# A DeltaNet and SwiGLU kernel: first diagonals with heads side by side, ScalarE's passes over the first weight piece ahead of its copies of N, and the last stores on two queues

## The chip, the cores and the metric

The kernel runs on one core of a Trainium2 chip. The metric is the device time of one execution in microseconds; lower is better. A core has five engines that run side by side and meet only through semaphores: TensorE (PE, with its weight loads PEld), VectorE (DVE), ScalarE (ACT), GpSimd (POOL) and SyncE (SP), which here only issues transfers. A transfer (DMA) is issued on the queue of SP, ACT or POOL and is carried by 16 shared DMA engines.

## The reference

A gated-delta-rule attention block feeds a SwiGLU feed-forward block. Only this matters here:

```python
k_n = k / (np.linalg.norm(k, axis=-1, keepdims=True) + 1e-06)     # q, k, v: (4, 8, 768, 48)
for t in range(S):
    y[:, :, t] = np.einsum('bhd,bhde->bhe', q[:, :, t], state)
    v_old = np.einsum('bhde,bhd->bhe', state, kt)
    state = state + bt[:, :, :, None] * np.einsum('bhd,bhe->bhde', kt, vt - v_old)
x = y.transpose(0, 2, 1, 3).reshape(3072, 384)
g = x @ w_gate                                                    # (384, 1536)
out = (g * (1.0 / (1.0 + np.exp(-g))) * (x @ w_val)) @ w_out      # (1536, 384)
```

Inputs q, k, v and beta are float32, the three weight matrices are float64, and the output is float32.

## The kernel before

The sequence is cut into 12 chunks of 64 tokens. Inside a chunk the recurrence is turned into matrix products: the Gram matrices of the k rows (and of q with k) on TensorE, a triangular inverse, and products with the state, which is carried from chunk to chunk. With a batch of 4 and 8 heads there are 32 matrices of 64 by 64 in a chunk, 16 in each half of the partitions. A matrix is cut into blocks of 32 rows, and the inverse is built from blocks: the diagonal blocks are inverted by a substitution on VectorE that steps through all heads together, and the blocks below the diagonal come in through matrix products with a matrix called N.

The start. The order of the instructions on each engine is the order of the program from line 1929 on; nothing is reordered by a scheduler. Chunks 0 and 1 are treated apart:

- `load_k(0)` and `load_k(1)` (line 190) put half of each transfer on SP's queue and half on ACT's. All other loads are on SP's queue, apart from beta's eight small ones on POOL's (`load_beta`, line 406).
- `norms` (line 381) squares and sums the k rows on VectorE and takes the root on POOL. Between the square and the sum of chunk 0 stands a memset of `qpad[0]`'s padding (line 388). `load_q(0)`, the first transfer of SP's queue behind the k rows of chunks 0 and 1, writes `qpad[0]` and so waits for that memset. Behind it on SP's queue stand k of chunks 2 and 3, q of 1, v of 0, q of 2, and then the weight pieces.
- `turned` (line 461) transposes a chunk's rows on TensorE into PSUM; ScalarE copies them to SBUF (line 488 or 490).
- `first_gram` (line 639) makes the Gram matrices of a chunk, 32 products of 64 columns, into two PSUM banks, one for each parity of the head. In a bank the 512 columns of a row are x (which 32 of the 64 columns), then the head, then i, so that the 32 columns of one head lie side by side. For chunk 1 the two banks are those that its transposes came out of.
- `first_diag` (line 650) picks the diagonal blocks: ScalarE multiplies the first half by a row mask (line 654), VectorE adds the second half with another (line 656). They go to `first_of["flat"]`, where the 32 columns of one i hold all heads of both chunks; an element of one head is thus written 32 elements (128 bytes) behind the last.
- VectorE transposes `flat` (line 1951), which is what `first_substitution` (line 691) works on, 30 instructions in a row. `first_z` (line 710) transposes the result back, `spread_z` (line 715) spreads it with one ScalarE instruction and three VectorE ones (lines 725 and 727), and `n_products` (line 729) makes N from it on TensorE (line 735).
- `low_copies` (line 665) copies the blocks below the diagonal from the same PSUM banks with 12 ScalarE instructions (line 669).
- `unread` (line 635) runs products that nobody reads, to keep TensorE busy while it would wait. Four of them (line 968 of the program) stand ahead of `n_products`.
- `first_advance` (line 942) is the recurrence's step for chunk 0: N's products, N's copies (`n_copies`, line 739, with lines 741 and 749), three chained products with N (line 954), the outputs of chunk 0, and at its end ScalarE's copy of the first state (line 1050). Chunk 1's step starts with a product on that state (line 1152).

The weights. They arrive as 64-bit numbers in pieces of 256 (later 512 or 384) columns, staged by `stage` (line 253) on SP's queue. Most of the first 18 pieces wait, by a copy of one column on POOL (line 261), for an earlier piece to have landed. `power_step` (line 266) makes two ScalarE passes over a piece (lines 274 and 280), and `convert` (line 284) three VectorE operations, which give the float32 values. `power_step(0)` stands behind the first step of `first_advance` (line 1993), so ScalarE makes its passes over piece 0 behind its copies of N and of the first products.

The rest. From chunk 2 on the feed-forward block of one chunk runs on TensorE while the next chunk's recurrence is fitted in between. `output_fast` (line 1667) makes the output of a chunk and stores the two halves of its tokens with `store` (line 1608), two transfers each on SP's queue. The last chunk's stores end the kernel.

Of the kernel before, what the change touches and what calls it, by code (L numbers as in the profile page):

```python
# [14 lines left out]
DP = 64  # L15
R = 32
# [4 lines left out]
def kernel(  # L21
# [25 lines left out]
    nc = tc.nc  # L47

    B, H, S, D = q.shape
    NCH = S // C  # L50
# [7 lines left out]
    HH = NB * H  # L58
# [38 lines left out]
    qpad = [const.tile([128, NB, H, DP], FP32, name=f"qpad{i}") for i in range(QB)]  # L97
# [283 lines left out]
    def norms(c):  # L381

        ksq = work.tile([128, NB, H, D], FP32, name="ksq", tag="r", bufs=2)
        x = knp[c][:, :, :, 0:D]
        nc.vector.tensor_tensor(out=ksq, in0=x, in1=x, op=ALU.mult)
        n = n_t[0][:, c].rearrange("p (par bp j) -> p par bp j", par=2, bp=NB)
        if c == 0:
            nc.vector.memset(qpad[0][:, :, :, D - 1 : DP], 0.0)
        ksq_v = ksq.rearrange("p bp (j par) d -> p par bp j d", par=2)
        for par in range(2):  # L390
            nc.vector.tensor_reduce(
                out=n[:, par], in_=ksq_v[:, par], axis=mybir.AxisListType.X, op=ALU.add
            )
        n = n_t[0][:, c]
        nc.gpsimd.tensor_tensor(out=n, in0=n, in1=half[:, 0:HH], op=ALU.pow)
# [58 lines left out]
    def banks(name, tag):  # L454

        if type(tag) is int:
            return [ps_ffn([128, 512], name, tag + i) for i in range(2)]
        p = ps_pair(name, tag)
        return [p[:, 0], p[:, 1]]

    def turned(c, of_q, tag=None):

        if tag is None:
            tag = "py" if of_q else "px"
        x = qpad[c % QB] if of_q else kn_of(c)
        if of_q:
            xt = work.tile([128, NB * NJ * 2 * C], FP32, name="qt", bufs=1)
        else:
            xt = kt_of(c)
        if c >= blocks_of[of_q][1]:  # L470
            xt_v = xt.rearrange("p (b bp j i) -> p bp j b i", bp=NB, b=2, j=NJ)
            (qt if of_q else kt)[c] = xt_v
            blocks = blocks_of[of_q][2]
            nc.vector.transpose(xt, blocks.rearrange("p bp h d -> p (bp h d)"))
            spent.append(1.8)
            if c + 1 < NCH:
                for par in range(2):
                    late_loads.append(lambda par=par: load_blocks(of_q, c + 1, (par,)))
            return
        xt = xt.rearrange("p (bp j b i) -> p bp j b i", bp=NB, j=NJ, b=2)  # L480
        (qt if of_q else kt)[c] = xt
        p_t = banks("p_t", tag)
        for bp in range(NB):
            for j in range(NJ):
                at = slice(128 * j, 128 * j + 128)
                nc.tensor.transpose(p_t[bp][:, at], x[:, bp, 2 * j : 2 * j + 2], ident)
            if type(tag) is int:
                nc.scalar.copy(xt[:, bp].rearrange("p j b i -> p (j b i)"), p_t[bp])
        for bp in range(NB if type(tag) is not int else 0):
            nc.scalar.copy(xt[:, bp].rearrange("p j b i -> p (j b i)"), p_t[bp])  # L490
        if of_q and c + QB < Q_BLOCKS:
            load_q(c + QB)
# [109 lines left out]
    first_of, l_sb, n_sb = {}, {}, {}  # L602
# [7 lines left out]
    def first_tiles():  # L610
        a = work.tile([128, C * 2 * HH], FP32, name="a_sb")
        for c in range(2):
            l_sb[c] = a[:, R * R * c : R * R * (c + 1)].rearrange(
                "p (h k) -> p h k", k=C
            )
        first_of["flat"] = new_mb().rearrange("p k i -> p (k i)")
        first_of["diag"] = first_of["flat"].rearrange("p (j h) -> p h j", j=R)
        first_of["zb"] = places["z1"].bitcast(FP32)[:, 4 * H_ - 1056 : 4 * H_]
        first_of["mb"] = places["wo"].bitcast(FP32)[:, 2 * H_ : 2 * H_ + 1056]
        nc.vector.memset(first_of["zb"], 0.0)  # L620
        for c in range(2):
            nc.vector.memset(l_sb[c][:, :, 48:C], 0.0)
        for x, rows in enumerate((slice(16, C), slice(R, C), slice(48, C), slice(0, R))):
            nc.vector.tensor_reduce(
                out=m_two[:, x],
                in_=ident.rearrange("p (b n) -> p b n", b=2)[:, :, rows],
                axis=mybir.AxisListType.X,
                op=ALU.add,
            )
        nc.vector.tensor_tensor(  # L630
            out=m_rows, in0=m_two[:, :, 0], in1=m_two[:, :, 1], op=ALU.add
        )
        nc.vector.tensor_scalar_mul(m_low, m_rows[:, 0:3], -1.0)
# [5 lines left out]

    def first_gram(c, tag):  # L640

        p_v = [p.rearrange("p (x h i) -> p x h i", x=2, i=R) for p in banks("p_g", tag)]
        for bp, j, par, b, _ in every():
            k_v = kt[c][half_of(par), bp, j, b].rearrange("p (x i) -> p x i", x=2)
            nc.tensor.matmul(
                p_v[par][half_of(b), :, NJ * bp + j], kt[c][half_of(par), bp, j, b], k_v
            )
        return p_v

    def first_diag(c, p):  # L650
        to = first_of["diag"][:, HH * c : HH * c + HH]
        to = to.rearrange("p (par h) j -> p par h j", par=2)
        for par in range(2):
            nc.scalar.mul(to[:, par], p[par][:, 0], m_rows[:, 3:4])
        for par in range(2):
            nc.vector.scalar_tensor_tensor(
                out=to[:, par],
                in0=p[par][:, 1],
                scalar=m_rows[:, 1:2],
                in1=to[:, par],  # L660
                op0=ALU.mult,
                op1=ALU.add,
            )
# [943 lines left out]

    def store(c, bp, o_sb):
        for b in range(2):
            nc.sync.dma_start(  # L1610
                out=out_v[NB * b + bp, c * C : (c + 1) * C],
                in_=o_sb[half_of(b)],
            )
# [172 lines left out]
    def step(kind, fn, *args):  # L1786
        key = (kind, args or (1,))
        if key not in gens:
            gens[key] = [fn(*args), 0]
        if next(gens[key][0], None) != MORE:  # L1790
            gens[key][1] += 1
# [128 lines left out]
    with tc.manual_schedule(  # L1920
# [8 lines left out]
        new_n(0)  # L1929
        load_beta()  # L1930
        first_tiles()
        norms(0)
        norms(1)
        load_q(0)
# [5 lines left out]
        unread(3, ps_pair("p_t", "px")[:, 0])  # L1940
        turned(0, False, 0)
        p_g = [first_gram(0, "px")]
        first_diag(0, p_g[0])
        turned(1, False, 2)
        p_g.append(first_gram(1, 2))
        first_diag(1, p_g[1])
        spread_beta(copy_a)
# [41 lines left out]
        new_nt(0, spare_of_q, state_flat[:, LEAD : LEAD + 512])  # L1989
        new_nt(1, zb_1.rearrange("p k i -> p (k i)"), spare_of_q[:, 0:512])  # L1990
        gens["advance", (0,)] = [first_advance(), 0]
        step("advance", advance, 0)
        power_step(0)
        step("advance", advance, 0)
        converts_first(0)
        power_step(2)
# [110 lines left out]
```

## Time and profile before

| what | value |
|---|---|
| median of 3 runs | 663.73 us (663.14 to 665.0) |
| the profiled execution, its own time | 662.01 us |
| its span (first to last instruction) | 660.3 us |
| TensorE busy | 647.3 us, 98% of the span |
| VectorE, ScalarE, GpSimd busy | 476.7, 281.5, 198.5 us |
| mean granted clock of TensorE | 0.997 |
| granted clock from 32.9 to 36.2 us | 0.50 |
| transfers | 68.57 MB, mean 104 GB/s |

The profiled execution is one run, and 1.72 us faster than the median of the three that were timed. Times in the views are microseconds from the start of its span. A line of the timeline has the start, the busy time, the engine, the source line, the operation, the tile written and the tile read, the shape and the number of instructions merged; in brackets stands how long the engine had been idle and what ended that. "issue" means that the profile shows nothing that was waited for. SPq and ACTq are the times in which an engine issues a transfer. TensorE's float32 products are made in two passes, so that the profile has two records of a product and two of its weight load.

### The profile page before, as it was taken

How to read it: one execution, taken by the hardware profiler on the slowest of the kernel's cores; microseconds unless marked ns; L12 is line 12 of the kernel's file. 1: busy time of each engine (PE TensorE's matmuls, PEld its weight loads, DVE VectorE, ACT ScalarE, POOL GpSimd, SP SyncE). 2: the span in 40 equal slices, each digit the busy share in tenths (PEclk: the TensorE clock that was granted, in tenths of full speed). 3: DMA queues.
4: the chain of work that ended last, by engine and by line, in shares of the span. 5: the costliest groups of instructions: out<-in, count | busy, mean ns of one | idle time of the engine just before them, and what ended most of it. 6: DMA issues, size and time to landing. Idle time of an engine off the chain costs nothing.

```text
span 660.3 us, 24914 instructions
## 1 busy us (share of the span) xinstructions
PE 647.3 (98%) x10856; PEld 595.8 (90%) x10856; DVE 476.7 (72%) x991; ACT 281.5 (43%) x626; POOL 198.5 (30%) x310
## 2 busy tenths in 40 slices
PE   8899999999999999999999999999999999999997
PEld 4568888767999999999999999999999999999997
DVE  6879799999688767758667758677758655655562
ACT  5788867124336433434433433532333433334230
POOL 7130041023894032880031881031881000000000
PEclk9999999999999999999999999999999999999999
DMA  9668762005742551373454274363363442222321
GB/s 135 142 173 272 205 164 101 1 14 99 195 81 69 103 117 51 93 140 84 104 127 88 61 164 92 85 135 98 72 136 85 100 105 66 62 94 66 87 66 25
DMA packets 147438, 68.57 MB, mean 104 GB/s; under 512 B 123456, under 2 KB 126560, under 8 KB 147328
## 3 DMA queue, kind: packets, MB, share of 16 engines
q1 hardware_dynamic: 144992, 66.48, 42.6%
q8 instruction: 85, 1.39, 0.8%
q10 hardware_dynamic: 2080, 0.39, 0.4%
q0 software_dynamic: 256, 0.10, 0.1%
q14 instruction: 25, 0.20, 0.1%
HBM read 59.08 MB, written 7.86 MB: 101 GB/s over the span
## 4 chain that ended last, share of the span: by engine, by line
PE 85%; DVE 6%; DMA 4%; SPq 2%; issue 1%; ACT 1%; POOL 0%; DVEq 0%; ACTq 0%; POOLq 0%
PE ffn L1407 40%; PE ffn L1683 21%; PE ffn L1564 8%; DMA h_f<-in_moe_w_val_dram 3%; PE ffn L1593 2%; PE p_px L1169 2%; SPq L139 2%; PE p_py L502 1%; DVE x_t L587 1%; DVE zb L593 1%; PE p_py L1071 1%; PE p_px L1152 1%; PE p_py L1088 1%; PE p_px L502 1%; PE p_px L923 1%
## 5 line engine op out<-in xcount | busy, mean ns | idle before, releaser
L1407 PE MATMUL ffn<-x_t,w_gv 128*128 128x128 f32 x800 | 108.7, 279 | 0.8 <-DVE p_sb L1633 0.7
L1407 PEld LDWEIGHTS ffn<-x_t,w_gv 128*128 128x128 f32 x800 | 97.4, 192 | 3.9 <-DVE p_sb L1633 1.8
L1441 ACT ACTIVATE sil<-ffn 128x256 f32<-128x256 f32 x100 | 36.4, 383 | 115.4 <-PE ffn L1407 109.3
L1407 PE MATMUL ffn<-x_ffn,w_gv 128*128 128x128 f32 x640 | 84.6, 275 | 0.0
L1683 PE MATMUL ffn<-wo_sb,h_f 128*128 128x192 f32 x480 | 83.9, 328 | 0.0
L1683 PEld LDWEIGHTS ffn<-wo_sb,h_f 128*128 128x128 f32 x480 | 77.9, 190 | 0.6
L1407 PEld LDWEIGHTS ffn<-x_ffn,w_gv 128*128 128x128 f32 x640 | 78.0, 192 | 0.3
L822 POOL TENSOR_TENSOR n_b<-mb,half 128x32 f32<-128x32 f32 x5 | 27.6, 5520 | 159.2 <-DVE mb L556 159.2
L587 POOL TENSOR_TENSOR h_f<-zb,mb 128x31 f32<-128x31 f32 (+15 forms) x124 | 69.3, 559 | 19.2 <-PE p_py L800 6.0
L593 POOL TENSOR_TENSOR zb<-zb,h_f 128x31 f32<-128x31 f32 (+15 forms) x124 | 70.6, 569 | 9.7
L1407 PE MATMUL ffn<-x_t,h_f 128*128 128x128 f32 x472 | 64.7, 280 | 0.0
L1407 PEld LDWEIGHTS ffn<-x_t,h_f 128*128 128x128 f32 x472 | 57.3, 192 | 1.6 <-DVE ffn L1633 0.5
L1442 DVE TENSOR_TENSOR h_f<-sil,ffn 128x256 f32<-128x256 f32 x100 | 39.3, 418 | 23.8 <-ACT sil L1441 23.8
L1103 ACT COPY x_ffn<-p_py 32x256 f32<-32x256 f32 (+3 forms) x108 | 39.3, 364 | 29.0 <-PE p_py L1088 27.3
L1633 DVE TENSOR_TENSOR ffn<-p_sb,ffn 128x512 f32<-128x512 f32 x40 | 27.8, 695 | 25.8 <-PE ffn L1407 25.1
L1636 DVE TENSOR_TENSOR ffn<-ffn,p_sb 128x512 f32<-128x512 f32 x40 | 27.5, 691 | 19.9 <-PE ffn L1407 19.1
L1683 PE MATMUL ffn<-last_k,h_f 128*128 128x192 f32 x200 | 36.0, 327 | 0.0
L1636 DVE TENSOR_TENSOR o_sb<-o_sb,ffn 128x192 f32<-128x192 f32 x50 | 17.5, 350 | 24.2 <-PE ffn L1683 23.7
L1564 PE MATMUL ffn<-x_t,w_gv 128*128 128x256 f32 x144 | 33.9, 385 | 0.2 <-DVE x_t L1045 0.2
L1683 PEld LDWEIGHTS ffn<-last_k,h_f 128*128 128x128 f32 x200 | 32.9, 190 | 0.1
L1564 PE MATMUL ffn<-x_ffn,w_gv 128*128 128x256 f32 x144 | 31.9, 380 | 0.0
L1407 PE MATMUL ffn<-x_ffn,h_f 128*128 128x128 f32 x232 | 30.9, 276 | 0.0
(330 smaller groups left out, 1172.7 us busy)
## 6 DMA issues: line engine op xcount, KB each, us to landing
h_f<-w_s SPq DMA_DIRECT2D x81, 256.0 KB, 2.8
more_w<-w_s SPq DMA_DIRECT2D x27, 256.0 KB, 2.8
vin<-in_v_dram SPq DMA_DIRECT2D x48, 96.0 KB, 3.5
out_dram<-o_sb SPq DMA_DIRECT2D x48, 96.0 KB, 2.2
kn<-in_k_dram SPq DMA_DIRECT2D x20, 192.0 KB, 4.7
zt<-in_moe_w_out_dram SPq DMA_DIRECT2D x10, 384.0 KB, 4.3
qpad<-in_q_dram SPq DMA_DIRECT2D x36, 64.0 KB, 3.0
w_s<-h_f SPq DMA_DIRECT2D x7, 256.0 KB, 2.8
```

What stands on the lines that cost most here:

```text
L139: dmas[b % len(dmas)].dma_start(out=t[64 * b : 64 * b + 64, :, :, 0:D].rearrange("p bp h d -> p (bp h) d"), in_=halves(x, c, b).rearrange( ...
L587: engine.tensor_tensor(out=t_v, in0=zb[:, 0 : j + 1, j : j + 1].to_broadcast([128, j + 1, m]), in1=mb[:, j : j + 1, j + 1 : R].to_broadcas ...
L593: engine.tensor_tensor(out=zb[:, 0 : j + 1, j + 1 : R], in0=zb[:, 0 : j + 1, j + 1 : R], in1=t_v, op=ALU.add,)
L822: nc.gpsimd.tensor_tensor(out=n, in0=mb.rearrange("p j i -> p (j i)")[:, 0 : R * R : R + 1], in1=half, op=ALU.pow,)
L1103: nc.scalar.copy(x_all[at % 128 : at % 128 + rows, at // 128].rearrange("p (bp b i) -> p bp b i", bp=NB, b=2), p[64 * half + lo : 64 * hal ...
L1407: nc.tensor.matmul(p[:, u], w(u), moving, start=start and u == 0, stop=True, skip_group_check=True,)
L1441: nc.scalar.activation(silu_of, p[:, 0:2], ACTF.Silu)
L1442: nc.vector.tensor_tensor(out=h_of(c, PAIRS[r][e % 3], e // 3), in0=silu_of, in1=p[:, 2:4], op=ALU.mult)
L1564: nc.tensor.matmul(ps[name][:, i], w_sb[:, t, (f + i) * 128 : (f + i + 1) * 128], xts[c][:, t], start=(t == 0 and i == 0), stop=(t == KT - 1),
L1633: nc.vector.tensor_tensor(out=out, in0=a, in1=b, op=ALU.subtract)
L1636: nc.vector.tensor_tensor(out=out, in0=a, in1=b, op=ALU.add)
L1683: nc.tensor.matmul(p[x, part], a(f - f % 2)[:, f % 2], b(f), start=not begun and f == 0, stop=f == FH - 1, skip_group_check=True,)
```

## The change

There are five edits:

1. The memset of `qpad[0]`'s padding goes from the middle of `norms(0)` to a place ahead of it, behind `first_tiles`.
2. `first_gram` puts the columns of a bank in the order x, i, head: the heads lie side by side, and the 64 columns of one product lie 8 elements (32 bytes) apart. `first_diag` walks over i and then over heads, so it reads PSUM in a row and writes runs of 8 elements. `low_copies` is not edited, but reads elements that now lie 32 bytes apart.
3. `first_diag` of chunk 0 takes a function that it calls between its two ScalarE instructions: the transposes of chunk 1 with their two ScalarE copies. On TensorE the order stays; on ScalarE the copies stand behind the first of the two instructions instead of behind both.
4. `power_step(0)` goes ahead of the first step of `first_advance`: ScalarE's two passes over piece 0 stand ahead of its copies of N.
5. In the last chunk, one of the two transfers of each `store` goes to ACT's queue.

```diff
@@ norms
-        if c == 0:
-            nc.vector.memset(qpad[0][:, :, :, D - 1 : DP], 0.0)
@@ first_tiles
-        first_of["diag"] = first_of["flat"].rearrange("p (j h) -> p h j", j=R)
@@ first_gram
-        p_v = [p.rearrange("p (x h i) -> p x h i", x=2, i=R) for p in banks("p_g", tag)]
+        p_v = [p.rearrange("p (x i h) -> p x h i", x=2, i=R) for p in banks("p_g", tag)]
@@ first_diag
-    def first_diag(c, p):
-        to = first_of["diag"][:, HH * c : HH * c + HH]
-        to = to.rearrange("p (par h) j -> p par h j", par=2)
+    def first_diag(c, p, between=None):
+        to = first_of["flat"].rearrange("p (j c par h) -> p c par j h", c=2, par=2, j=R)
+        to = to[:, c]
+        p = [p_h.rearrange("p x h j -> p x j h") for p_h in p]
         for par in range(2):
             nc.scalar.mul(to[:, par], p[par][:, 0], m_rows[:, 3:4])
+            if between and par == 0:
+                between()
@@ store
-            nc.sync.dma_start(
+            queue = nc.scalar if c == NCH - 1 and b == bp else nc.sync
+            queue.dma_start(
@@ the program
         first_tiles()
+        nc.vector.memset(qpad[0][:, :, :, D - 1 : DP], 0.0)
         norms(0)
...
-        first_diag(0, p_g[0])
-        turned(1, False, 2)
+        first_diag(0, p_g[0], lambda: turned(1, False, 2))
...
         gens["advance", (0,)] = [first_advance(), 0]
+        power_step(0)
         step("advance", advance, 0)
-        power_step(0)
         step("advance", advance, 0)
```

## The prediction

> **What bounds the kernel now.** First the page's busy shares, then what the TensorE waits for after 48.3 us, then each engine's busy time by stretch.
>
> ```profile
> span 660.3 us, 24914 instructions
> PE 647.3 (98%) x10856; PEld 595.8 (90%) x10856; DVE 476.7 (72%) x991; ACT 281.5 (43%) x626; POOL 198.5 (30%) x310
> ```
>
> ```profile
> PE p_px L1152 <- ACT state L1050: 0.3, 1, 0.3
> ```
>
> ```profile
> 31.00:32.60 1.60, 0.01 (x2) 0.00 (x0) 0.06 (x1) 1.42 (x4) 0.13 (x1) 1.00 0.52 147
> 32.90:36.20 3.30, 3.30 (x124) 3.24 (x117) 2.58 (x4) 1.99 (x6) 3.10 (x4) 0.50 0.50 140
> ...
> 48.30:656.50 608.20, 606.68 (x9856) 568.91 (x9856) 439.02 (x894) 248.19 (x548) 178.40 (x269) 1.00 0.42 101
> ```
>
> The last fence has the stretch, its length, the busy time of PE, PE's weight loads, DVE, ACT and POOL, the granted clock, the DMA share and GB/s. From 48.3 to 656.5 PE idles 1.5 us in 608. The change alters no instruction in that stretch, so it can act in two places alone: what comes before L1152 starts at 48.30, and what follows the last product. Before 48.30 three strands meet at L1050, ScalarE's copy of the first state: the compute chain, the weight pieces, and PE's own order. Here are the chain of waits and the timeline of that time.
>
> ```profile
> 6.60 0.30 DVE qpad L388
> ...
> 6.91 0.60 SPq L139
> ...
> 23.38 4.62 DMA h_f<-in_moe_w_val_dram
> ...
> 48.30 1.15 PE p_px L1152 x64
> ```
>
> ```profile
> 9.49 1.11 ACT L488 COPY kt<-ffn 128x512 f32<-128x512 f32 x2
> ...
> 11.85 1.17 ACT L654 ACTIVATE mb<-ffn,m_rows 128x256 f32<-128x256 f32 x2 [1.25 <-PE ffn L645]
> ...
> 12.59 1.32 DVE L656 SCALAR_TENSOR_TENSOR mb<-ffn,m_rows,mb 128x256 f32<-128x256 f32 x2 [1.08 <-ACT mb L654]
> ...
> 13.95 1.25 DVE L1951 STREAM_TRANSPOSE wo_sb<-mb 128x1024 f32<-128x1024 f32 x1
> 14.25 1.67 ACT L669 ACTIVATE a_sb<-p_px,m_low 128x128 f32<-128x128 f32 x6
> ...
> 23.79 3.63 PE L638 MATMUL ffn<-half 128*32 128x512 f32 x8
> ...
> 28.08 1.16 PE L735 MATMUL ffn<-zt,a_sb 64*64 64x64 f32 x64 [0.66 <-ACT zt L725]
> ...
> 32.63 0.73 PE L954 MATMUL p_px<-v,qpad 64*64 64x48 f32 x22 [1.62 <-issue]
> ...
> 46.14 0.44 ACT L274 ACTIVATE w_gv<-h_f 128x256 f32<-128x256 f32 x1 [0.49 <-DMA h_f<-in_moe_w_val_dram]
> ...
> 654.59 3.12 SPq L1610 DMA_DIRECT2D out_dram<-o_sb  x4
> ```
>
> The reader sees: SP's queue stands until the memset of qpad (L388) and then works back to back to the first weight pieces; the diagonals (L654, L656) feed the transpose L1951, from which the substitution runs straight to L735, where PE waits 0.66 us behind dummies (L638) that ended at 27.42; and ScalarE waits 0.49 us for a piece right before L1050.
>
> **The memset moved ahead of the norms.** VectorE idles from the end of m_low (3.48) until the first k rows (5.63), which covers its 0.29 us (if not, ksq starts 0.29 late). SP can then issue load_q(0) at about 3.8 in place of 6.91, and behind it k(2), k(3), q(1), v(0), q(2) and pieces 0 and 1, 16 transfers in all. The lead is between 0 (SP issues up to 2.5 us each there, so rings hold it back) and 3.1. The DMA share is 1.4 to 1.5 from 3 to 7 us, 0.33 in 7:8 and 0.68 in 8:9; filling those two to 1.5 gives (1.17+0.82)/1.5 = 1.3 us, which I take. Beta's eight small loads on POOL's queue (3.96 to 7.54) get company; L425 needs them only at 11. Worth: the 0.49 us before L274 at 46.14, and a limit of 1.3 on what the start can win.
>
> **kt copies between the two halves of the first diagonal.** kt of chunk 1 started at 9.49 behind two L654 (starts 8.52, 9.04). Behind one: 8.52+0.36 (below) = 8.88, but the transposes end at 9.47, so the second copy starts at 9.52 and ends at 10.12 instead of 10.60. The gram of chunk 1 shifts by -0.48.
>
> **The diagonals' new layout.** L654 issues every 0.50 us for 256 elements written 128 bytes apart; L274, 256 elements written in a row, every 0.34; L669 every 0.25 for 128. I take 0.36. L656 takes 0.71 with strided operands, L682 (same operation and size, runs of 16) 0.43. From 11.85-0.48 = 11.37: second L654 at 11.73, lasting 0.47, last L656 at 12.27, ending 12.70. L1951 starts at 12.73 instead of 13.95: -1.2. POOL's power (to 13.71) is needed only behind L1951. So L725 ends at 26.83 and L735 could start at 26.88.
>
> **Dearer low copies.** L669 now reads PSUM 32 bytes apart. No row has that. Low end: nothing. High end: L725, ScalarE's read 128 bytes apart of SBUF, 753 ns for 256 and 1180 for 512, 1.67 ns an element; contiguous ones (L741 585 for 512, L979 478 for 384) 0.84. That is 0.83x128 = 0.107 us each, 1.28 for 12. The operation is L669's, the step is nearer L725's, so I take the middle, 0.64. These copies stand on ScalarE ahead of the kt, a_sb, qt copies, whose grams precede the dummies: these end at 27.42-0.48+0.64 = 27.58 (26.94 to 28.22). L735 starts there, since that is later than 26.88: -0.48 (-1.14 to +0.14).
>
> **Strided writes of the grams.** L645 writes 64 columns in two runs of 32, then 32 bytes apart. Low end 0; high end each gram doubles from 1.18 us, as nothing in the trace doubles more (L954 from 0.68 to 1.08 at half the clock). In a gram one bank and half gets a 64-column record every fourth time, 74 ns, far from L1407's 132 ns for 128 on one target, so I take 0.
> The Trainium skill's "PSUM — Partial Sum Buffer", Specifications, says that any non-contiguous access pattern slows matmuls significantly (8-byte lines). By the rows above the sum stays; by that rule the first rival holds.
>
> **ScalarE's passes over piece 0.** L274 and L280 (0.75 us, 31.70 to 32.45) go ahead of L741. Behind them wait the copy of N and the v copies, which PE's second product needs. ScalarE ends L522 near 27.8, the passes 28.55, N's products 28.8, so the copy is not late; piece 0 (POOL's copy shows it landed by 27.42, then about 26.1) is there. Cost 0; if the piece were 1 us later than before, the copy would be about 0.6 late. Gain: VectorE's L293 starts 1.7 us earlier, with nothing on the path behind it. PE's pause until 32.63 has no semaphore ("issue"): four products had run, and pauses without one end at 32.63, 36.63 and 46.02, 256 and 768 PE records apart, which is the page's instruction queue (85 fetches for 21,712 records, 255 each). So I give it nothing.
> The Trainium skill's "Runtime: NRT & Kernel Launch", Instruction fetch mechanics, gives the same 256 and calls crossing a block mostly hidden; by that word the pause would be the passes', the fifth case below.
>
> **The last stores.** Four issues of 0.53 us, 2.1 us to landing; the last starts at 657.11. Halves issued together gain at most 0.53, at least 0 (they share the DMA engines); I take 0.35.
>
> **Sum.** PE strand: L1564 ahead of L1152 ended at 47.96, now 47.48. ScalarE strand: L1050 ended at 48.26, less 0.49 and 0.48: 47.29. So L1152 at 47.48, -0.82; stores -0.35: -1.17. Span 660.3-1.2 = 659.1; the profiled run took 662.01, 1.72 under the median of 663.73, so 660.8 for such a run and 662.6 for the median. What this kernel's measurement tells from no change is about 0.3%, 2.0 us (its three runs spread 1.9).
>
> **Rivals.**
> 1. Grams slowed by strided PSUM writes (slower): gram 0 at +1.18 holds back PE's transposes of chunk 1, gram 1 adds 1.18, so dummies end at 27.58+2.36 = 29.94, L735 +1.9, L1152 at 49.8, +1.5; with stores +1.2: 664.9 (with dear low copies 665.5). It decides from 0.58 us a gram (then -0.82+1.16 = +0.35). For: the new step of 32 bytes. Against: the 74 ns.
> 2. Low copies cost nothing extra: L735 -1.14, capped by the pieces' 1.3 at L1050: -1.3-0.35: 662.1. For: PSUM is not SBUF. Against: L654's and L725's strides both cost 0.8 ns an element.
> 3. No lead: SP's rings are full anyway, pieces land as before, and L1050 stays. Only the stores: 663.4. For: issues of 2.5 us at 12.42. Against: the dip at 7 to 9 us.
> 4. The q rows collide with the k rows of chunk 1 (landed at 8.2): one more transfer ahead, 1.2 us; then L735 +0.6: about +0.1 in all, 663.8.
> 5. The pause was the passes': PE goes on 1.6 us earlier and keeps its clock (half from 32.9 to 36.2). For: they end at 32.45. Against: DVE's restart follows that by 0.09, PE's by 0.18. Limited by the pieces' lead (1.3 to 3.1): -1.7 to -3.4, say 661.4.
>
> **How the numbers follow.** Forecast 0.45 (its own range 661.6 to 663.6), rivals 0.14, 0.18, 0.10, 0.05, 0.08. Faster means below 661.7: rival 5 (0.08), a third of rival 2, where the lead is longer than 1.3 (0.06), and the spread of runs under the forecast and the rest of 2 (0.08): 0.22. Slower means above 665.7: the dear half of 1 with another half-clock window (0.07) and the spread over 1, 3 and 4 (0.08): 0.15. Same: 0.63. Range 660.6 to 665.2.
>
> **What would show it.** load_q(0) issued near 3.8 and pieces 1.3 us earlier; L654 near 0.36 apart, L656 near 0.43; L669's spacing between 0.25 and 0.36; L645's 64 records still 1.18 us; L735 near 27.6; a PE pause still ending about 4.2 us after L735 starts; no DMA wait before L274 at 46; L1152 near 47.5; the last landing 0.35 earlier behind the last product. Wrong if L645 grows, L735 moves later than 28.1, or L1152 does not move.

## The result, and the profile after

| | executions | median us | ratio to before, 95% interval |
|---|---|---|---|
| kernel before, beside the first comparison | 12 | 664.84 | |
| changed kernel, first comparison | 12 | 662.12 | 0.9964 [0.9948, 0.9981] |
| changed kernel, second comparison | 12 | 663.81 | 0.9987 [0.9966, 1.0008] |

The two lots of the changed kernel together have a mean of 663.28 us (24 executions, standard deviation 1.80); the kernel before has 664.81 over the 110 executions that were timed beside all the kernels of this study (standard deviation 1.50). The difference is -1.53 us, and with the two standard errors (0.37 and 0.14) its 95% interval is -0.75 to -2.3 us, that is -0.11% to -0.35%. The two lots of the changed kernel (a lot is the executions of a kernel that were timed together) differ by 1.47 us, about twice the standard error of that difference, so this interval, which takes all executions as independent, is rather too narrow. The forecast was -1.17 us.

The profiled execution of the changed kernel took 661.65 us. First the page, then its busy time in three of the stretches shown of before, with the same columns.

```profile
span 659.9 us, 24915 instructions
PE 646.2 (98%) x10856; PEld 594.8 (90%) x10856; DVE 476.6 (72%) x991; ACT 280.9 (43%) x626; POOL 198.4 (30%) x310
```

```profile
31.00:32.60 1.60, 0.45 (x30) 0.45 (x32) 1.56 (x2) 0.01 (x1) 1.60 (x2) 1.00 0.57 135
32.90:36.20 3.30, 1.81 (x96) 1.47 (x88) 2.66 (x6) 2.91 (x9) 0.83 (x3) 1.00 0.72 126
48.30:656.50 608.20, 606.51 (x9833) 568.63 (x9824) 438.81 (x894) 246.99 (x546) 178.10 (x267) 1.00 0.41 100
```

The stretch from 32.9 to 36.2 ran at a granted clock of 0.50 before and runs at 1.00 now, though TensorE is idle for 1.49 of the 3.30 us. The dense stage is dense still. The timeline of the start (in the changed file L654, L645, L638, L425, L1951 and L1636 have become L652, L642, L635, L423, L1952 and L1637):

```profile
3.48 0.28 DVE L1933 MEMSET qpad<- 128x272 f32 x1
3.79 2.45 SPq L139 DMA_DIRECT2D qpad<-in_q_dram  x2
...
11.60 1.38 PE L423 MATMUL p_py<-wo_sb,ident 16*32 16x192 f32 x16
11.71 0.84 ACT L652 ACTIVATE mb<-ffn,m_rows 128x256 f32<-128x256 f32 x2 [0.88 <-PE ffn L642]
12.22 0.88 DVE L656 SCALAR_TENSOR_TENSOR mb<-ffn,m_rows,mb 128x256 f32<-128x256 f32 x2 [0.47 <-ACT mb L652]
13.13 1.25 DVE L1952 STREAM_TRANSPOSE wo_sb<-mb 128x1024 f32<-128x1024 f32 x1
...
24.11 3.63 PE L635 MATMUL ffn<-half 128*32 128x512 f32 x8
27.67 1.16 PE L735 MATMUL ffn<-zt,a_sb 64*64 64x64 f32 x64
...
32.15 0.51 PE L954 MATMUL p_px<-v,qpad 64*64 64x48 f32 x21 [1.88 <-issue]
...
47.74 1.15 PE L1152 MATMUL p_px<-state,kt 48*64 48x48 f32 x64
```

Two L652 now take 0.84 together and two L656 0.88, where they took 1.17 and 1.32. Six low copies (L669) take 1.67 as before (from 14.56). Beta's products (L423) take 1.38 where they took 0.93. L735 comes 0.41 earlier, and L1152 0.56 earlier. TensorE's pause without a named cause is still there, 1.88 instead of 1.62. Behind L1152 the pair of traces gives back nearly all: at 55.9 TensorE pauses where it did not before, and the last product ends 0.08 earlier. The last stores win what is left of the 0.4: from the last product's end to the end of the span it is 3.89 in place of 4.17. They are now issued on two queues:

```profile
654.52 2.49 SPq L1611 DMA_DIRECT2D out_dram<-o_sb  x2
654.52 2.52 ACTq L1611 DMA_DIRECT2D out_dram<-o_sb  x2
```

So one pair of traces says -0.4, the first comparison -2.7 (of medians) and the second -0.9. Both profiled executions were faster than their kernel's median. The experiments had to show what an ordinary execution does, as well as what each edit is worth.

### The profile page after: what moved, and what is told of

It is laid out like the page before. It is cut to its first block, busy times and chain, and to the rows that moved or that the text cites. A ratio compares the mean times of both kernels' runs of the same rounds, so it can differ in the third digit from the quotient of the medians.

```text
span 659.9 us, 24915 instructions
## 1 busy us (share of the span) xinstructions
PE 646.2 (98%) x10856; PEld 594.8 (90%) x10856; DVE 476.6 (72%) x991; ACT 280.9 (43%) x626; POOL 198.4 (30%) x310
## 4 chain that ended last, share of the span: by engine, by line
PE 91%; DVE 4%; ACT 2%; issue 1%; DMA 1%; SPq 0%; DVEq 0%; ACTq 0%
PE ffn L1407 42%; PE ffn L1684 21%; PE ffn L1564 9%; PE ffn L1593 2%; PE p_px L1169 2%; PE p_px L500 2%; PE p_py L1071 1%; PE p_py L500 1%; PE p_px L923 1%; PE p_px L1152 1%; DVE x_t L585 1%; DVE zb L591 1%; PE p_py L1088 1%; DMA kn<-in_k_dram 1%; PE p_py L905 1%
## 5 line engine op out<-in xcount | busy, mean ns | idle before, releaser
L822 POOL TENSOR_TENSOR n_b<-mb,half 128x32 f32<-128x32 f32 x5 | 27.6, 5518 | 160.0 <-DVE mb L554 160.0
L1634 DVE TENSOR_TENSOR ffn<-p_sb,ffn 128x512 f32<-128x512 f32 x40 | 27.8, 695 | 26.0 <-PE ffn L1407 25.3
L1637 DVE TENSOR_TENSOR ffn<-ffn,p_sb 128x512 f32<-128x512 f32 x40 | 27.5, 692 | 20.2 <-PE ffn L1407 19.3
L1637 DVE TENSOR_TENSOR o_sb<-o_sb,ffn 128x192 f32<-128x192 f32 x50 | 17.5, 351 | 24.1 <-PE ffn L1684 23.7
L1684 PEld LDWEIGHTS ffn<-last_k,h_f 128*128 128x128 f32 x200 | 32.9, 190 | 0.1
```

What stands on the lines that cost most here:

```text
L822: nc.gpsimd.tensor_tensor(out=n, in0=mb.rearrange("p j i -> p (j i)")[:, 0 : R * R : R + 1], in1=half, op=ALU.pow,)
L1634: nc.vector.tensor_tensor(out=out, in0=a, in1=b, op=ALU.subtract)
L1637: nc.vector.tensor_tensor(out=out, in0=a, in1=b, op=ALU.add)
L1684: nc.tensor.matmul(p[x, part], a(f - f % 2)[:, f % 2], b(f), start=not begun and f == 0, stop=f == FH - 1, skip_group_check=True,)
```

## The experiments

From here on "mean" is that of the executions of one kernel. TensorE's instructions are fetched on the queue that the profile calls "instruction": 85 fetches for 21,712 records, about 255 at a time. Such a part is called a block here, and a pause of TensorE where one begins a block pause. "Dummies" are the unread products ahead of L735.

### The kernel before, unchanged

No edit; a second profile, and the granted clock of twelve executions (each execution comes with its mean clock).

> The kernel before, unchanged, for a second profiled execution and for the noise. Ratio 1.000 within 0.2%. The first profiled execution took 662.01 us, 2.8 under its kernel's median, so it was a quick one. Theory A, the ordinary execution loses its time ahead of L1152: this profile has a span of about 662 to 664, L1152 starts as much later than 48.30 as the span is above 660.3, and more of TensorE's pauses at instruction blocks or a longer half-clock stretch lie before it. Theory B, the time is lost in the dense stretch: L1152 near 48.3 and more than 607.8 us from there to the last product.

Measured: ratio 0.9995 [0.9971, 1.0019]; the profiled execution took 665.47, its span was 663.8 and its mean clock 0.992. L1152 started at 50.34 in place of 48.30. Windows of its trace, with the columns as above:

```profile
29.80:33.22 3.42, 1.64 (x98) 1.42 (x92) 1.63 (x4) 2.56 (x6) 0.35 (x2) 1.00 0.59 179
33.22:36.63 3.41, 3.13 (x115) 3.00 (x108) 2.80 (x5) 2.32 (x6) 3.04 (x4) 0.50 0.47 119
36.63:40.04 3.41, 3.21 (x78) 2.31 (x81) 2.78 (x7) 1.48 (x4) 0.26 (x1) 0.50 0.77 173
40.04:43.46 3.42, 3.42 (x63) 2.52 (x56) 1.07 (x3) 1.83 (x6) 0.48 (x3) 0.50 0.31 85
```

The stretches are windows of 3.413 us, counted from where the clock record changes. In the first, TensorE is busy 1.64 of 3.42 us, because of the 1.66 us pause. Then the clock is halved for three windows of 3.413 us and comes back after the first one in which TensorE was busy throughout (3.42). In the first profile of this kernel the first half-clock window was already fully busy (3.30 of 3.30 in 32.90:36.20), so it had one window and not three.

So theory A holds for 2.04 of the 3.5 us: the first profile, on which the prediction was summed, was a quick one by luck. The remaining 1.4 us lie behind L1152 (609.26 against 607.82 to the last product), 0.93 of them in one pause at 58.4.

### The changed kernel, once more

No edit either.

> The changed kernel once more, for a second profile and for the share of half-clock windows. Theory (two parts: 1.2 us of path, and about one half-clock window of 0.9 us fewer): ratio 0.995 to 0.998, mean clock 0.997 to 0.999 against 0.995 of the kernel before; at equal clock 1.0 to 1.6 us under it. Rival (the first comparison was lucky; only the path is won): mean clock 0.9955 as before, ratio 0.998.

Measured: ratio 0.9987 [0.9966, 1.0008], mean 664.01, mean clock 0.9969 (0.9982 in the first comparison). The ratio lies a little above what was expected and the clock at its lower edge; the rival's clock of 0.9955 did not come, its ratio nearly did. The trace has L1152 at 48.02, no pause at 32 (where the block at record 1201 begins), one of 1.28 at 35.9 (record 1457) and one of 1.09 at 57.2 (record 2479), and two half-clock windows. The first comparison was on the lucky side, and the two lots are taken together below.

### One part of the change undone

Four of the five edits were each undone alone. The third, chunk 1's copies between the halves of the first diagonal, was not, so what it is worth by itself stays open.

**Memset back behind the first norms**

```diff
         first_tiles()
-        nc.vector.memset(qpad[0][:, :, :, D - 1 : DP], 0.0)
...
+        if c == 0:
+            nc.vector.memset(qpad[0][:, :, :, D - 1 : DP], 0.0)
```

> The changed kernel with the memset of qpad back behind the first norms. Theory lead (the earlier transfers free L1050): load_q(0) issued near 6.9, piece 0 and 1 last bytes 1.2 to 1.6 us later than 24.50 and 26.42, the wait before L274 at 46 back with 0.3 to 0.5, L1152 at 48.0 to 48.3, time 0.4 to 0.6 us above the changed kernel (ratio to before about 0.997). Rival (TensorE's instruction blocks set L1152): L1152 stays within 0.2 of 47.74, ratio 0.9964. On top: the kn rows of chunk 1 land 0.4 us earlier again (L385's second start 8.69 back to 8.28) and beta's products (L423) take 0.93 again instead of 1.38, so the dummies (L635) start near 23.3 instead of 24.11.

Measured: ratio 0.9959 [0.9937, 0.9981], the lowest mean of the four kernels run together (662.40). L735 stood at 27.02, earlier than in any kernel with the early memset, and beta's products took 0.92 again. The expected price at L1050 was there: TensorE waited 1.53 us for it at 47.55. It is larger than the 0.3 to 0.5 that were expected. And still the kernel was not slower. Here are its timeline's lines (two more lines above them, so L737 is L735 and L1154 is L1152):

```profile
27.02 1.16 PE L737 MATMUL ffn<-zt,a_sb 64*64 64x64 f32 x64
...
30.32 0.51 PE L956 MATMUL p_px<-v,qpad 64*64 64x48 f32 x21 [0.45 <-issue]
...
47.55 1.15 PE L1154 MATMUL p_px<-state,kt 48*64 48x48 f32 x64 [1.53 <-ACT state L1052]
```

Because that contradicted the lead, it was run again, with a theory of its own.

> The changed kernel with the memset back behind the first norms, once more: its first lot had the lowest mean of all (662.4; the changed kernel's two lots 662.55 and 664.0). Theory collision (the memset's move costs as much as it brings): mean 662.4 to 663.3, ratio to before 0.996 to 0.9975, not above the changed kernel. Theory lead (its move is worth 0.5): mean 663.8 or more, ratio 0.998 or above.

Measured: ratio 0.9954 [0.9938, 0.9970], mean 662.18. Over both lots the mean is 662.29 (25 executions, standard deviation 1.46), 0.99 us under the changed kernel, interval 0.07 to 1.9. The memset's move does not pay in the changed kernel; it costs, probably about 1 us, though the interval nearly reaches zero. What it delays is seen in the transfers of beta. This is the view of the tile that beta is loaded into, first of the changed kernel, then of the kernel with the memset back:

```profile
L423 PE MATMUL p_py<-wo_sb,ident x16: 317/321/345, 11.6 to 12.7; 16*32 16x192 f32 x16
...
DMA to landing us min/median/max: 4.9/5.1/6.0
```

```profile
L425 PE MATMUL p_py<-wo_sb,ident x16: 318/321/345, 11.3 to 11.9; 16*32 16x192 f32 x16
...
DMA to landing us min/median/max: 2.7/3.9/5.8
```

The last line is the time from issue to landing of beta's eight small loads. With the q rows on the DMA engines ahead of them, none lands in under 4.9 us. The last packet of beta's queue moves at 10.9 instead of 8.7, L423 trickles from 11.6 to 12.7, and TensorE's later work on this strand moves with it: the dummies started at 24.11 to 25.39 in the eight traces with the early memset and at 23.45 to 24.09 in the six without it.

That this delay is the 1 us is not shown. In the two traces with the memset back L1152 started at 47.55 and 49.23, no earlier than the changed kernel's 47.74 and 48.02, and both of these executions (663.48 and 666.63 us) were longer than the kernel's mean.

**Old layout of the diagonals**

```diff
-        p_v = [p.rearrange("p (x i h) -> p x h i", x=2, i=R) for p in banks("p_g", tag)]
+        p_v = [p.rearrange("p (x h i) -> p x h i", x=2, i=R) for p in banks("p_g", tag)]
...
-        to = first_of["flat"].rearrange("p (j c par h) -> p c par j h", c=2, par=2, j=R)
-        to = to[:, c]
-        p = [p_h.rearrange("p x h j -> p x j h") for p_h in p]
+        to = first_of["flat"].rearrange("p (j h) -> p h j", j=R)
+        to = to[:, HH * c : HH * c + HH]
+        to = to.rearrange("p (par h) j -> p par h j", par=2)
```

> The changed kernel with the diagonals' old layout (grams write rows in runs, diagonals written 128 bytes apart); kt copies still between. L652 0.50 apart again, L656 0.70; the transpose L1952 starts 0.8 to 1.0 later than 13.13. Theory (the layout brings L735 forward only until the dummies end): L735 at 27.9 to 28.1 instead of 27.67, and of these 0.3 us at most 0.2 arrive at L1152; ratio 0.996 to 0.997. Rival (the layout is what the gain is made of): L1152 0.8 or more later and the ratio at 0.998 or above.

Measured: ratio 0.9969 [0.9948, 0.9991], mean 663.57, 0.3 above the changed kernel's two lots and well inside the noise. The transpose started at 13.80 instead of 13.13 and L735 at 28.03, as the first theory said; but the dummies ended at 28.10 in this trace, so L735 waited for them and not for the transpose. L1152 started at 48.29, 0.55 later than in the changed kernel's first profile, which is more than the first theory allowed and less than the rival asked. No gain from the layout can be measured; the interval of the 0.3 (-0.7 to 1.2) does not rule one out.

**Last stores on one queue**

```diff
-            queue = nc.scalar if c == NCH - 1 and b == bp else nc.sync
-            queue.dma_start(
+            nc.sync.dma_start(
```

> The changed kernel with all last stores on SyncE's queue again. From the end of the last product to the end of the span 4.14 us instead of 3.81; nothing else moves. Time 0.3 us above the changed kernel, ratio about 0.997. Rival (the two queues matter more in ordinary executions than in the profiled pair): 1 us or more, ratio 0.998 or above.

Measured: ratio 0.9969 [0.9946, 0.9991]. In its trace it is 4.18 us from the last product's end to the end of the span. Over all fourteen traces this is 4.15 to 4.18 with one queue and 3.89 to 3.96 with two. The edit is worth 0.25 us, and it touches nothing ahead of the last chunk. Its twelve executions gave a mean of 663.35, 0.07 above the changed kernel's two lots: a quarter of a us can be read from the traces, but not from twelve executions.

**Passes over piece 0 behind the copies of N**

```diff
-        power_step(0)
         step("advance", advance, 0)
+        power_step(0)
         step("advance", advance, 0)
```

> The changed kernel with ScalarE's passes over piece 0 behind its copies of N again. Theory blocks (prediction's step, worth nothing): L735 27.5 to 28.1, the pause still ends about 4.5 us behind L735's start at record 1201, time within 0.5 of the changed kernel (ratio 0.9955 to 0.997). Rival passes (their place is what keeps the clock): the pause is 1 us or more longer, mean clock falls from 0.998 to 0.996 or less, ratio 0.998 or more.

Measured: ratio 1.0002 [0.9981, 1.0022], mean clock 0.9952 (0.9976 over the changed kernel's 24). That was the rival's number, by a way that neither theory had: the pause at the block was not longer, but 0.15 us. Behind it two other waits opened. The timeline:

```profile
31.47 2.54 POOL L539 TENSOR_TENSOR p_sb<-p_sb,mask_q 128x512 f32<-128x512 f32 x2
...
31.57 0.41 ACT L280 ACTIVATE h_f<-h_f 128x256 uint32<-128x256 uint32 x1
31.90 0.46 ACT L990 COPY uu<-p_px 128x384 f32<-128x384 f32 x1
...
32.08 0.80 DVE L293 TENSOR_SCALAR h_f<-w_gv 128x256 uint32<-128x256 uint32 x1 [1.47 <-POOL h_f L261]
...
32.41 0.25 PE L954 MATMUL p_px<-uu,qpad 64*64 64x48 f32 x1 [0.74 <-ACT uu L990]
...
32.91 1.38 DVE L301 SCALAR_TENSOR_TENSOR w_gv<-w_gv,h_f 128x256 uint32<-128x256 uint32 x1
34.33 0.42 DVE L313 CUSTOM_DVE_ANT_0 w_gv<-w_gv,h_f 128x512 uint16<-128x512 uint16 x1
34.78 0.56 DVE L1637 TENSOR_TENSOR x_t<-v,p_px 128x384 f32<-128x384 f32 x1
...
35.39 0.79 PE L954 MATMUL p_px<-x_t,qpad 64*64 64x48 f32 x32 [1.83 <-DVE x_t L1637]
```

The first is on ScalarE: its copy L990 starts only behind the second pass L280, and TensorE waits 0.74 us for it. The second is on VectorE. Its three operations on piece 0 (L293, L301, L313) can start only behind ScalarE's passes, which are late again and end at 31.98 (the POOL copy that the row of L293 names had ended at 31.51). Two of them run beside POOL's long product L539 and take 0.80 and 1.38 us instead of the 0.29 and 0.43 that they take elsewhere. The sum L1637 stands behind them on VectorE and starts 0.03 us after them, and TensorE waits 1.83 us for it. The window with both waits was busy 0.46, and the next one ran at half clock.

Because the step had been priced at nothing, this undo was run again and the edit was also tried alone on the kernel before.

> The changed kernel with ScalarE's passes over piece 0 behind its copies of N again, once more. Theory slot: ratio to before 0.999 to 1.001 and mean clock near 0.995 to 0.996 as in its first lot (1.0002). Prediction's step (worth nothing): ratio 0.9965 to 0.998 as the changed kernel's.

Measured: ratio 0.9991 [0.9972, 1.0010], mean clock again 0.9952. Over both lots the mean is 664.78 (24 executions, standard deviation 1.81), 1.50 us above the changed kernel, interval 0.5 to 2.5, and 0.03 us under the kernel before. Without this one edit, the other four together win nothing that can be measured. Its trace shows the two waits again, but small ones, and a block pause:

```profile
32.55 0.25 PE L954 MATMUL p_px<-uu,qpad 64*64 64x48 f32 x1 [0.43 <-ACT uu L990]
...
34.08 0.33 PE L954 MATMUL p_px<-x_t,qpad 64*64 64x48 f32 x8 [0.38 <-DVE x_t L1637]
...
35.91 0.88 PE L954 MATMUL p_px<-x_t,qpad 64*64 64x48 f32 x22 [1.50 <-issue]
```

L1637 again starts right behind L313 (33.47 after 33.43), but here L539 had ended before L293 began, the three operations took 0.29, 0.43 and 0.42, and TensorE waited only 0.38 us. That is little more than the 0.28 in both traces of the changed kernel, in the second of which L1637 also starts right behind L313 (33.67 after 33.61). So the long wait for VectorE is seen in one trace; together the waits and the block pause left TensorE 0.45 busy in the window before the clock halved.

### One part of the change alone

> The kernel before with one edit: ScalarE's passes over piece 0 ahead of its copies of N. Theory slot (undoing this edit alone cost 2 us, 665.2 against a mean of 663.3 for the two lots of the changed kernel: the earlier passes free piece 0's slot, the pieces of L1050's passes land 1 to 2 us earlier, and L1050 no longer waits): piece 0's passes at 28.5 to 29.0 in place of 31.7, the wait before the last passes ahead of L1050 gone, mean of the times 1 to 2 us under the kernel before (ratio 0.997 to 0.9985). Prediction's step (worth nothing): ratio 0.9995 to 1.0005, and the 2 us of the undo were spread of the half-clock windows.

Measured: ratio 0.9992 [0.9974, 1.0009], mean 664.44, mean clock 0.9943. Piece 0's passes stood at 29.07 as expected, L1152 at 48.66, and the gain of 1 to 2 us was not there. In the kernel before VectorE's queue is not what TensorE waits for in this stretch: in both profiles of it VectorE itself waits for TensorE's product ahead of the sum (0.38 and 0.28 us), and the trace with this edit shows the block pause (1.30 us, window busy 0.58), two windows of half clock, and VectorE idle 2.78 us ahead of the sum. Alone the edit wins nothing that can be measured (-0.4, interval -1.2 to 0.5).

> The kernel before with one edit: the memset of qpad ahead of the norms. Prediction's step (pieces 1.3 earlier, the wait of 0.49 before L1050 gone, at most 0.5 of gain): ratio 0.999 to 1.000. Theory collision (the earlier q rows hold up the k rows of chunk 1 by 0.4 and beta's rows, so the low copies, the dummies and L735 come 0.3 to 0.6 later): L735 at 28.3 to 28.7, ratio 1.000 to 1.0015.

Measured: ratio 0.9998 [0.9979, 1.0017], mean 664.63 over eleven executions (a twelfth took 671.49), mean clock 0.9934, the lowest of all. The dummies started at 24.61 (23.79 before), the first and last of beta's products at 11.52 and 13.17, L735 at 28.18. The delays came as the theory of the collision said, if a little short of its L735, and the time as the prediction's step did. The profiled execution, at 661.11, was the fastest of all and had no half-clock window. Alone the edit wins or costs nothing that can be measured.

### TensorE's instruction blocks moved

From 25 to 60 us of the traces so far, all but one of TensorE's pauses of over 0.3 us without a named cause stood at the same places in its record count: 947, 1201, 1457, 1713, 1967 and 2479, multiples of 256 apart within two records. To move these, four unread products of 512 columns were made into 32 of 64, nearly the same TensorE time (4.04 us for 3.63, pause left out) in 112 records more.

```diff
-        unread(4, banks("p_t", 2)[0])
+        unread(32, banks("p_t", 2)[0], 64)
```

> The kernel before, with the four unread products of 512 columns ahead of L735 (dummies, L638) made into 32 of 64 columns: the same time of TensorE, 112 instruction records more. Theory blocks (TensorE pauses where its 256-record blocks begin, at records 945, 1201, 1457, 1713, 1967, 2479 of every trace so far; a pause that leaves a window of 3.41 us under about 0.55 busy brings half clock, until a window is wholly busy): the pauses keep these record numbers and so fall 112 records earlier in the program; block 945 begins in the dummies near 25 us, so the pause of 1.6 us in the v,qpad products (31.0 to 32.6) is gone or under 0.6, the mean clock rises from 0.995 to 0.997 or more, and the time falls by 0.8 to 2 us (ratio 0.997 to 0.9985). Rival passes (the pause is of ScalarE's passes over piece 0): the pause stays ahead of the same products, ratio 1.000.

> The changed kernel with the same 32 small unread products in place of four large ones. Theory blocks: no pause of 1.9 in the v,qpad products at 30.3; the next blocks begin 112 records earlier in the program and cost up to 1.5 us where the uu products begin; half-clock windows as few as or fewer than in the changed kernel (mean clock 0.998 or more); L1152 at 46.9 to 47.7; 0 to 1.3 us under the changed kernel, ratio to before 0.9945 to 0.9965. Rival passes: the pause before the v,qpad products stays, ratio 0.9964.

Measured: ratios 1.0071 [1.0043, 1.0100] over eleven executions and 1.0087 [1.0057, 1.0118] over six. From the timeline of the second:

```profile
27.96 4.43 PE L635 MATMUL ffn<-half 128*32 128x64 f32 x47 [2.07 <-issue]
32.32 1.16 PE L735 MATMUL ffn<-zt,a_sb 64*64 64x64 f32 x64
...
343.05 0.83 PE L1407 MATMUL ffn<-x_ffn,more_w 128*128 128x128 f32 x6 [1.61 <-issue]
```

The place of the pause is as the block theory said: it left the v,qpad products, and a pause now sits in the dummies at record 947, of 2.07 us here and 1.11 in the other. Nothing in the data waits there, so the pause belongs to the record count and not to ScalarE's passes. The price was wrong, and in sign: the means are 4.8 and 7.9 us above those of the kernels that were edited. All later blocks were shifted too. Pauses of 0.5 to 1.8 us appeared near 340 and 440 us in both traces, at the same three records (11,901, 15,204 and 15,460; the first at 343.05 here), where none of the other twelve traces has one of 0.2; from L1152 to the last product it took 612.9 and 616.8, against 607.8 to 611.8 elsewhere. These three pauses add up to 3.6 and 3.9 us, so they are the larger part of the loss in the one kernel and half of it in the other. In the kernel before, the shift did bring L1152 forward, from 48.30 to 47.20, and lost it many times over afterwards; in the changed kernel L1152 came at 50.29, over 2 us later than in its two profiles without the shift (47.74 and 48.02), where 46.9 to 47.7 was expected.

### Half clock over all executions

Each execution has its mean granted clock, and at full clock otherwise, (1 - clock) x 2 x span is the time spent at half clock. Its mean over executions: 6.4 us for the kernel before (12; 6.8 over the 98 others that were timed beside the experiments), 3.2 for the changed kernel (24), 2.6 with the memset back (25), 6.4 with the passes back (24), 7.5 and 8.8 for the passes and the memset alone (12 and 11). A straight line through these kernels' executions and those with the old layout and with one queue, with an own level for each lot, gives 1.0 us (interval 0.8 to 1.2) for each 3.41 us at half clock. The line cannot part the half clock from the pauses that go before it. By it the 3.2 us less of the changed kernel are worth about 1.0 us of its 1.5, and the rest, about 0.5, is left for path and stores.

## Why the prediction was right in size, and where its steps failed

**The forecast.** 662.6 us, -1.17, against a measured -1.53 (-0.75 to -2.3), with the first comparison's median at 662.12. The size is right; the terms that made it up are not. That the sum came out near is luck: an edit that was given nothing was worth about 1.5, and one that was credited with a gain cost about 1.

**The base.** "the profiled run took 662.01, 1.72 under the median" was turned into a constant to add. It was not a constant but half-clock windows and block pauses that ordinary executions have more of. That cost in the kernel before (6.4 us of half clock on average, one window of 3.4 in the profile) was the larger part of what was won (about 1.0 of 1.53), and the sum had no term for it. Only rival 5 and the spread of the first rival named the half clock.

**"So it can act in two places alone".** This step failed. The change alters no instruction from L1152 to the last product, but that stretch took 607.82 and 609.26 us in the two profiles of the kernel before and 608.31 and 609.79 in those of the changed one. The sum forecast 0.82 at L1152 and carried it to the end. Of the 0.56 that came there in the first pair, 0.36 had gone at the pause at 55.9, and 0.08 arrived at the last product.

**The passes over piece 0: "Cost 0 ... nothing on the path behind it".** This step failed. What stands behind the passes on ScalarE is the copy L990, and behind VectorE's L293 the sum L1636, one stage further on; TensorE waits for both as soon as the block pause is short. The edit was worth 1.5 us (0.5 to 2.5) in the changed kernel, by the straight line mostly through half clock, and nothing measurable alone. Rival 5 had the edit right and the mechanism wrong: the pause itself is the blocks', as the prediction said, since it moved with the record count. How the 1.5 come about is not settled: of the two traces with the passes back one has 0.74 and 1.83 us of these waits, the other 0.43 and 0.38 and a block pause of 1.50, and an edit that frees either queue in another way was not tried.

**The memset's lead: "Worth: the 0.49 us before L274".** This step failed too. The signs came: load_q(0) was issued at 3.79 (3.8 forecast), piece 1's last bytes moved at 26.42 instead of 27.58, and the wait before L274 was gone. But the loads that got company were dismissed in one sentence ("L425 needs them only at 11"). The last of them then landed 2.2 us later (12.00, and 9.77 with the memset back), and the products on beta held up TensorE's strand. It is rival 4's mechanism, given 0.05, with beta's rows as the main victim: the k rows of chunk 1 were late by 0.41 (L385's second start, 8.28 to 8.69), beta's by more. Net cost about 1.0 (0.07 to 1.9) in the changed kernel and nothing measurable alone; how beta's delay becomes a us at the end is not shown.

**The copies between the diagonals and the layout.** The second diagonal of chunk 0 did start between, but the late k rows ate most of the shift: the gram of chunk 1 moved by 0.13 (10.65 to 10.52), not 0.48. L652 are 0.38 apart (0.36 forecast) and L656 0.40 (0.43). L1952 starts at 13.13 (12.73).

**The low copies, 0.64.** Mis-sized: they cost nothing, with twelve at 0.25 us spacing as before. That was rival 2's condition, and its gain did not show because the dummies were late for another reason, beta: they ended at 27.74 (27.58 forecast), and L735 started at 27.67 (27.6), right by two errors, which is luck. With the memset back L735 started at 27.02 and 27.19, near rival 2's 26.94 (28.08 less 1.14).

**Strided writes of the grams, 0.** Right: 64 records in 1.18 us in both layouts. The Trainium skill's "PSUM — Partial Sum Buffer", Specifications, has any non-contiguous access slow matmuls significantly; here 64 columns written 32 bytes apart took no longer than in two runs of 32, and rival 1 fell with it.

**The pause at 32.63.** Right in its place in the first pair (it ends 4.5 us behind L735's start in both; over the other traces whose blocks were not moved, TensorE passes that record 2.7 to 5.5 us behind it), and right that ScalarE's passes are not its cause. The sentence of the Trainium skill's "Runtime: NRT & Kernel Launch", Instruction fetch mechanics, that crossing a block is mostly hidden does not hold in this stage of small products: 0 to 2.24 us per block in fourteen traces.

**The stores, -0.35.** 0.25 us, inside the bounds.

**Chances.** 0.63 on no change beyond 0.3% and 0.22 on faster: the two lots gave -0.36% and -0.13%, and both together -0.23%.

**A version that is probably better than both.** The changed kernel with the memset in its old place: 0.9959 and 0.9954 to the kernel before, in two lots. Why it stays faster although L1050 waits for pieces again is settled only in part: L735 is 0.5 to 1.9 us earlier in its two traces than in the changed kernel's two, but TensorE still waits there for ScalarE's last passes, 1.5 us in one of its traces and 3.7 in the other.

## What to carry to other kernels

When a profiled execution is faster than the median of the timed runs, what is missing from it is part of what a change can win: take a second profile and look at where the clock was granted, before summing on the first. A transfer that is moved ahead can be paid for by the ones it passes, here on ACT's and POOL's queues as on its own, and what waits for such small loads has to be followed to the end. An engine's own order is a path: before an edit is priced at nothing, read what stands behind the moved instruction on its own engine and on the engine that it feeds, and what that will be late for once the present wait is shorter.

## What the runs showed of the hardware

- **The clock is granted in windows of 3.413 us** whose phase to the start of the kernel differs from run to run. In the fourteen traces, 12 of 13 half-clock stretches ahead of the last product followed a window in which TensorE was busy 0.31 to 0.58 (the other one was busy 0.90); each lasted until the end of the first window that was busy throughout, one to three windows. Four windows of 0.50 to 0.56 went unpunished, and so did four of 0.43 to 0.51 at the end of the kernel, so the busy share alone does not decide. So block pauses of 1.62, 1.66 and 1.88 us were followed by one, three and no windows of half clock; the 1.88 was cut in two by the edge of a window. The Trainium skill's "TensorE: Matmul & The Clock Gate", Part 1, gives the same free-running window; it has the clock fall after an idle window, where these runs show it fall after windows that were a third to over half busy.
- **The fetch of a block of 256 TensorE records can wait for a weight piece.** In the first trace with the memset back, TensorE came to record 945 near 27.2 and the last packet of a piece ended at 27.26; the fetch's first packet moved at 27.98 and the pause at record 1201 was 0.45. In the changed kernel's profile TensorE came there near 27.8, a piece was in flight until 29.88, and the fetch moved at 29.89; the pause was 1.88. From the fetch's packet to the end of the pause it was 2.34 and 2.26 us. This is read from the traces; no run tried it by itself.
- **112 TensorE records more at 25 us cost 5 to 8 us of 664**, 3.6 and 3.9 of them in three pauses near 340 and 440 us that stood at the same records in both kernels. That these are block edges which now fall in a bad place is the reading; no run moved them again.
- **VectorE's operations on a piece took 0.80 and 1.38 us beside POOL's L539** and 0.29 and 0.43 without it. In the changed kernel's first profile two of them took 1.51 and 1.38 beside it, and VectorE still idled 0.57 us ahead of the sum.
